# Block-causal attention and a SoLU layer on one core: transposed probabilities by way of DRAM, the first batch element in two parts, loads of two pairs at once

## The chip, the core and the metric

The kernel runs on one core of a Trainium2 chip: TensorE (PE), VectorE (DVE), ScalarE (ACT), GpSimd (POOL) and SyncE (SP), each with its own queue of instructions, and 16 DMA engines that carry the transfers. Nearly all transfers are issued on SP's queue. The metric is the device time of one execution in microseconds. Before: a median of 732.68 us over three runs (730.88 to 734.18).

## The reference

```python
# attention: 8 batch elements, 8 heads, 576 positions, head size 64; float32
scores = scale * np.matmul(q, k.transpose(0, 1, 3, 2))
mask = block_i >= block_j                  # blocks of 64 positions
scores = np.where(mask, scores, -1000000000.0)
attn = np.exp(scores - max); attn = attn / (sum + 1e-09)
attn_out = np.matmul(attn, v)
# then each of 4608 tokens, x = the 8 heads side by side (512)
h = x @ w_in                               # 512 -> 1024
solu = h * softmax(h)
ln = (solu - mean) / np.sqrt(var + 1e-06) * g_ln
out = ln @ w_out                           # 1024 -> 512
```

## The kernel before

Work comes in two kinds. **Attention** is done for a pair of heads at a time, 32 pairs, four to a batch element. **MoE tiles** (the SoLU layer) take 128 tokens each, 36 tiles, four and a half to a batch element; a tile can start when the attention output of its tokens stands in `xt`.

A product of float32 numbers is split into a high and a low part (`qh`, `ql`; `xh`, `xl`; `wih`, `wil` and so on) and made of three matmuls (L515, L673, L733). For a pair: q and k are loaded (L432, eight transfers of 32 partitions, each 18 runs of 32 numbers), transposed on DVE in 32x32 blocks (L474) and split; scores go to PSUM (L515, L509), DVE takes the row maximum (L540), ACT the exponential into `pb` (L552), and rows are scaled by the reciprocal of their sum (L570 to L572, on whichever of three engines is planned). The product with v needs the probabilities transposed, `pt`. DVE transposes `pb` within 32x32 blocks (L579); what is left is to move blocks between groups of 32 partitions, and that is `place` (L581 to L584): sixteen transfers of 32 partitions, 3,200 bytes per partition, from `pb` to `pt`, both in SBUF. The product with v (L596) then reads `pt`. The first four pairs (`PEP`, `PEQ`) are transposed on PE instead (L461, L496), while the weights are prepared from their 64-bit words (`prep`, L341).

For a MoE tile: h on PE (L673), maximum, exponential and product on DVE and ACT (L679 to L681), centring by POOL or DVE (L683), and again a transposition: DVE transposes u in 32x32 blocks into `zb` (L703, reading every fourth number), `zb` is written to the DRAM tile `zd` (L704) and read back rearranged into `ct` (L705), split into `ch` and `cl` (L711 to L715) and multiplied with w_out (L733). Tiles 0 to 3 and 35 use PE's transposition.

The order of the instructions on every engine is fixed when the program is built. A planner (`Schedule`, L59) plays the operations through with durations that are written beside them, and at each step gives an engine the ready operation with the lowest key; keys are the pair's or the tile's number plus an offset from `PARAMS`. `pb`, `pt` and `vr` have two buffers each. Transfers wait in SP's queue in its order: one that must wait holds those behind it.

Of the kernel before, what the change touches and what calls it, by code (L numbers as in the profile page):

```python
# [11 lines left out]
F32 = mybir.dt.float32  # L12
# [19 lines left out]
NPT = 2  # L32
PEP = (0, 1, 2, 3)
PET, PEL = 4, 35
NQK = 1
XB = 3
PEQ = 4
SWITCH = 70.0
SLACK = 120.0
START = {"PE": 0.0, "ACT": 2930.0, "DVE": 0.0, "POOL": 2500.0, "SP": 560.0}  # L40
PARAMS = {
# [6 lines left out]
    "a_w": 189.2, "a_xh": -137.2, "a_xl": -269.8, "a_c": -179.5, "a_o": 359.2, "np": 32, "l0": -21.1,  # L48
    "a_cl": -237.6, "a_ai": 1.9, "aff": 91.5, "a_t3": -207.8, "a_cm": -19.8, "a_cg": 177.6, "a_sa": -259.0,
    "a_sa32": -169.6, "a_qh": 4.5, "a_kl": -157.5, "a_ch": -224.1, "a_chd": 241.9, "a_clo": -32.4,  # L50
    "ct0": -156.5,
# [7 lines left out]
class Schedule:  # L59
# [49 lines left out]
    def run(self):  # L109
# [20 lines left out]
        while events:  # L130
# [18 lines left out]
            for e in engs:  # L149
# [46 lines left out]
                if best.dma > 0.0:  # L196
                    done = dmafree = max(done, dmafree) + best.dma
# [9 lines left out]
def kernel(  # L207
# [43 lines left out]
    qz, kz, qt, kt = (sb(x, [S]) for x in ("qz", "kz", "qt", "kt"))  # L251
    kq = sb("kq", [P])
# [20 lines left out]
    ub = [sb(f"ub{i}", [DFF]) for i in range(2)]  # L273
# [4 lines left out]
    zd = dp.tile([P, DFF], F32, name="zd")  # L278
    ct = sb("ct", [4, NKO, 32])
# [55 lines left out]
    w_in_w = w_in.bitcast(U32).rearrange("(c p) (n t) -> p c n t", p=P, t=2)  # L335
    w_out_w = w_out.bitcast(U32).rearrange("(c p) (n t) -> p c n t", p=P, t=2)
# [3 lines left out]

    def prep(i, src, hi, lo, gcol, name, key):  # L341
        raw = ub[i % 2].bitcast(U32).rearrange("p (n t) -> p n t", t=2)
        T1, T2, T3 = wtmp[i % 2]
        kr_, k1, k2, k3 = ("ub", i % 2), ("w1", i % 2), ("w2", i % 2), ("ob", i % 2)
        op("SP", 640, lambda: SP.dma_start(raw, src), w=[kr_], key=key, tail=2700, dma=1270)
# [22 lines left out]
    op("SP", 500, lambda: SP.dma_start(gt, g_ln.rearrange("(c p) -> p c", p=P)), w=["gt"], key=K["w0"] + K["w1"] * 6, tail=2100)  # L368
    n = 0
    for hf in range(2):  # L370
        for c in range(NKI):
            s_ = slice(hf * 512, hf * 512 + 512)
            prep(n, w_in_w[:, c, s_, :], wih[:, c, s_], wil[:, c, s_], None, f"wi{c}_{hf}", K["w0"] + K["w1"] * n)
            n += 1
    for c in range(NKO):
        prep(n, w_out_w[:, c, :, :], woh[:, c, :], wol[:, c, :], gt[:, c : c + 1], f"wo{c}", K["w0"] + K["w1"] * n)
        n += 1

    ptc = [(0, 4), (4, 8), (8, 12), (12, 16), (16, 19), (19, 22), (22, 25)]
# [3 lines left out]
    groups = [  # L383
        ("S", [(2, 0), (0, 384)], [320, 448]),
        ("S", [(1, 0)], [192]),
        ("S", [(3, 0)], [448]),
        ("D", [LAST], None),
    ]
    order_u = [(h, i) for is_ in ((2, 0), (1,)) for h in range(2) for i in is_] + [(0, 3), (1, 3), LAST]
# [16 lines left out]
    def attention(p):  # L406
        b0, hp = divmod(p, NP)
        i = p % 2
        sfx = "32" if p < NP else ""
# [3 lines left out]
        peq = p < PEQ  # L413
        pep = p in PEP
        for nm, src, dst in (("kz", k, kz), ("qz", q, qz)):

            def load(nm=nm, src=src, dst=dst):
                dma = ACT if p == 0 and nm == "kz" else SP
                if peq:
                    for h in range(2):  # L420
                        dma.dma_start(
                            dst[:, 0:512].rearrange("p (c d) -> p c d", c=4)[:, :, 64 * h : 64 * h + 64],
                            src[b0, 2 * hp + h, 0:512, :].rearrange("(c p) d -> p c d", p=P),
                        )
                    r0 = 0 if nm == "kz" else 64
                    SP.dma_start(
                        kq[r0 : r0 + 64, :].rearrange("p (h d) -> p h d", h=2),
                        src[b0, 2 * hp : 2 * hp + 2, 512:576, :].rearrange("h p d -> p h d"),
                    )
                    return  # L430
                for g in range(4):
                    dma.dma_start(  # L432
                        dst[32 * g : 32 * g + 32, :].rearrange("p (g d) -> p g d", d=32),
                        src[b0, 2 * hp + g // 2, :, 32 * (g % 2) : 32 * (g % 2) + 32].rearrange("(g p) d -> p g d", p=32),
                    )

            op("SP", 1790 if peq else 2040, load, w=[nm] + [nm + "q"] * peq, key=(K["l0"] if p == 0 else p) + K["ld" + sfx], tail=1700, dma=1870)
# [346 lines left out]
```

## Time and profile before

| | |
|---|---|
| median of three runs | 732.68 us |
| the profiled execution | 730.28 us, of which the span is 728.5 us |
| busy: PE, DVE, ACT, POOL | 92%, 83%, 68%, 44% of the span |
| DMA queue of SP (q1) | 230,416 packets, 124.32 MB, 70.1% of 16 engines |
| placing transfers `pt<-pb` | 448 (28 pairs x 16), from 88.4 to 639.5 us |
| weights and transposition on PE | until 88 us; MoE matmuls begin at 82.4 us |

In the rows that follow, a group's columns are its line, engine, operation, output and input tiles and count, then busy time and the mean of one in ns, then the engine's idle time before it and what ended it. In a row of windows the columns are the stretch in us, its length, the busy time of PE, PE's weight loads, DVE, ACT and POOL with their instructions, the granted clock of PE, the busy share of the 16 DMA engines and what they moved in GB/s. SPq is SP's queue, which issues transfers. The recorded ends of matmuls are modelled, so that PE's busy time is rather too high than too low.

### The profile page before, as it was taken

The numbers are of one execution on the slowest core, as the hardware profiler recorded it, in microseconds if no ns is written. First come the engines' busy times: TensorE is split into PE (matmuls) and PEld (weight loads), VectorE is DVE, ScalarE is ACT, GpSimd is POOL, SyncE is SP. The second block draws the span as 40 slices with busy tenths as digits, with TensorE's granted clock in tenths as the row PEclk, the third lists the DMA queues.
The fourth block names the chain that finished last, engine by engine and source line by source line (L and its number), as shares of the span: only waits on it lengthen the run. The fifth ranks groups of instructions, "written<-read, shape, count | busy, mean of one in ns | idle before, by whom it ended". The sixth has DMA issues, their size and how long they took to land.

```text
span 728.5 us, 14348 instructions
## 1 busy us (share of the span) xinstructions
PE 671.1 (92%) x4543; PEld 528.1 (72%) x4543; DVE 607.4 (83%) x1262; ACT 495.3 (68%) x1265; POOL 322.5 (44%) x491
## 2 busy tenths in 40 slices
PE   7786968999999998999999999899899988999997
PEld 6566757777677776778777777677677766878886
DVE  6999999988888999789799888899888789755672
ACT  5989958877777777665777686578585658434342
POOL 3755744454444655244353654245454434214310
PEclk7899989999999999999999999999999999999999
DMA  9584676676788888888778888888787874543431
GB/s 236 130 175 118 150 178 117 126 170 146 161 201 201 205 196 193 198 192 210 182 193 197 203 196 173 190 199 196 193 209 178 190 197 110 170 151 130 145 131 57
DMA packets 231547, 125.49 MB, mean 172 GB/s; under 512 B 190640, under 2 KB 206512, under 8 KB 231472
## 3 DMA queue, kind: packets, MB, share of 16 engines
q1 hardware_dynamic: 230416, 124.32, 70.1%
q8 instruction: 36, 0.59, 0.4%
q10 hardware_dynamic: 1056, 0.26, 0.2%
q14 instruction: 39, 0.32, 0.2%
HBM read 52.96 MB, written 25.69 MB: 108 GB/s over the span
## 4 chain that ended last, share of the span: by engine, by line
PE 32%; DVE 23%; SPq 14%; DMA 12%; ACT 12%; issue 5%; POOL 1%; DVEq 0%; ACTq 0%; POOLq 0%
PE ps L733 12%; SPq L584 11%; PE ps L673 9%; PE ps L596 5%; DVE pb L579 5%; DVE nm L540 5%; DMA pt<-pb 4%; ACT pb L552 4%; PE ps L515 4%; DMA ct<-zd 3%; ACT pb L572 3%; SPq L432 2%; DVE ub L681 2%; DVE zb L703 2%; PE ps L509 1%
## 5 line engine op out<-in xcount | busy, mean ns | idle before, releaser
L552 ACT ACTIVATE pb<-ps,nm 128x384 f32<-128x384 f32 (+4 forms) x288 | 157.3, 561 | 69.6 <-DVE nm L540 54.2
L540 DVE TENSOR_REDUCE nm<-ps 128x1 f32<-128x384 f32 (+4 forms) x288 | 131.8, 506 | 0.3
L596 PE MATMUL ps<-pt,vr 128*64 128x128 f32 (+2 forms) x1664 | 104.3, 286 | 25.4 <-DMA pt<-pb 13.7
L596 PEld LDWEIGHTS ps<-pt,vr 128*64 128x64 f32 x1664 | 90.2, 146 | 46.9 <-issue 16.4
L572 ACT ACTIVATE pb<-pb,rz 128x128 f32<-128x128 f32 (+4 forms) x191 | 101.2, 595 | 25.4 <-DVE rz L563 23.0
L579 DVE STREAM_TRANSPOSE pb<-pb 128x1536 f32<-128x1536 f32 (+1 forms) x56 | 102.1, 1829 | 9.5 <-POOL pb L570 5.8
L570 POOL TENSOR_SCALAR pb<-pb,rz 128x384 f32<-128x384 f32 (+4 forms) x97 | 62.3, 652 | 71.3 <-DVE rz L563 30.4
L733 PE MATMUL ps<-woh,ch 128*128 128x512 f32 x288 | 81.6, 405 | 4.0 <-ACT pb L552 3.4
L673 PE MATMUL ps<-wih,xh 128*128 128x512 f32 x288 | 83.8, 413 | 0.2 <-ACT xh L648 0.2
L673 PE MATMUL ps<-wil,xh 128*128 128x512 f32 x288 | 79.4, 398 | 0.0
L733 PE MATMUL ps<-woh,cl 128*128 128x512 f32 x288 | 78.7, 395 | 0.0
L673 PE MATMUL ps<-wih,xl 128*128 128x512 f32 x288 | 78.6, 395 | 0.0
L733 PE MATMUL ps<-wol,ch 128*128 128x512 f32 x288 | 78.6, 394 | 0.0
L733 PEld LDWEIGHTS ps<-woh,ch 128*128 128x128 f32 x288 | 51.8, 188 | 20.2 <-ACT pb L552 5.6
L703 DVE STREAM_TRANSPOSE zb<-ub 128x1024 f32<-128x1024 f32 x31 | 62.5, 2017 | 2.6 <-POOL ub L683 1.4
L673 PEld LDWEIGHTS ps<-wil,xh 128*128 128x128 f32 x288 | 54.8, 190 | 13.0
L673 PEld LDWEIGHTS ps<-wih,xh 128*128 128x128 f32 x288 | 51.1, 190 | 17.3 <-issue 4.8
L673 PEld LDWEIGHTS ps<-wih,xl 128*128 128x128 f32 x288 | 54.3, 188 | 12.8
L733 PEld LDWEIGHTS ps<-woh,cl 128*128 128x128 f32 x288 | 54.3, 188 | 12.8
L515 PE MATMUL ps<-kh,qh 64*128 64x384 f32 (+3 forms) x256 | 57.8, 390 | 6.2 <-ACT pb L552 1.8
L733 PEld LDWEIGHTS ps<-wol,ch 128*128 128x128 f32 x288 | 54.2, 188 | 12.7
L712 POOL TENSOR_SCALAR ch<-ct 128x512 fp32r<-128x512 f32 x36 | 22.0, 620 | 90.0 <-DMA ct<-zd 77.0
(116 smaller groups left out, 1262.3 us busy)
## 6 DMA issues: line engine op xcount, KB each, us to landing
pt<-pb SPq DMA_DIRECT2D x448, 100.0 KB, 2.2
zd<-zb SPq DMA_DIRECT2D x31, 512.0 KB, 3.0
ct<-zd SPq DMA_DIRECT2D x31, 512.0 KB, 4.3
out_dram<-ob SPq DMA_DIRECT2D x36, 256.0 KB, 3.1
vr<-in_v_dram SPq DMA_DIRECT2D x64, 128.0 KB, 3.3
kz<-in_k_dram SPq DMA_DIRECT2D x112, 72.0 KB, 2.7
qz<-in_q_dram SPq DMA_DIRECT2D x112, 72.0 KB, 3.0
ub<-in_moe_w_in_dram SPq DMA_DIRECT2D x8, 512.0 KB, 4.2
```

The lines of the kernel that those rows point to most:

```text
L515: PE.matmul(PS(sps[h])[:, off : off + 128 * (i_ + 1)], w_[half[h], 128 * i_ : 128 * i_ + 128], x_[half[h], 0 : 128 * (i_ + 1)], start=n_ = ...
L540: op("DVE", t_dve(wid[u]), lambda sp=sp, off=off, u=u: DVE.tensor_reduce(out=nm_[u], in_=PS(sp)[:, off : off + wid[u]], axis=AX.X, op=ALU. ...
L552: ACT.activation(dst, src, AF.Exp, bias=nm_[u], accum_out=z_[zg][:, zc : zc + 1])
L570: op("POOL", 0.836 * nn + 243, lambda b=b, zg=zg, zc=zc: POOL.tensor_scalar(out=puv(pb, b, pep), in0=puv(pb, b, pep), scalar1=rz_[zg][:, z ...
L572: ("ACT", t_act(nn, 93), lambda b=b, zg=zg, zc=zc: ACT.activation(puv(pb, b, pep), puv(pb, b, pep), AF.Copy, scale=rz_[zg][:, zc : zc + 1] ...
L579: op("DVE", 1.058 * 128 * (s1 - s0) + 86, lambda s0=s0, s1=s1: DVE.transpose(pb[:, :, s0:s1, :], pb[:, :, s0:s1, :]), r=[("P", i, b) for b ...
L584: SP.dma_start(pt_[32 * r_ : 32 * r_ + 32, a_, :, :], pb[32 * a_ : 32 * a_ + 32, r_, :, :])
L596: PE.matmul(dst(PS(av)[half[h]]), vt[:, j, 64 * h : 64 * h + 64], pt_[:, a0:a1, sl, :], start=start, stop=stop)
L673: PE.matmul(o_, a_[:, c, :], w_[:, c, s_], start=(si == 0 and c == 0), stop=(si == 2 and c == NKI - 1))
L703: op("DVE", t_dve(DFF), lambda: DVE.transpose(zb.rearrange("p (r c i) -> p r c i", r=4, i=32), u.rearrange("p (c i r) -> p r c i", r=4, i= ...
L712: alts=[("POOL", 671, lambda c_=c_, h_=h_: POOL.tensor_scalar(out=h_, in0=c_, scalar1=1.0, scalar2=1.0, op0=ALU.mult, op1=ALU.mult), K["a_ ...
L733: PE.matmul(o_, a_[:, c, :], w_[:, c, :], start=(hf == 0 and si == 0 and c == 0), stop=(hf == 1 and si == 2 and c == 7))
```

## The change

1. *Transposed probabilities by DRAM.* `place` goes. In its stead four writes (`spill`) bring `pb`, 128 partitions wide each, to a DRAM tile `pd` (two buffers), in the order that `pt` needs, and one read brings the whole of it to `pt`, 12,800 bytes per partition. The read waits until the four writes have landed.
2. *Two-pair loads.* q and k of two pairs are loaded by four transfers of 36 runs instead of eight of 18; to make these regular, a pair is now made of heads `ha` and `ha + 2`, and rows of w_in are loaded in the order that fits. DVE transposes them in place.
3. *First batch element in two parts.* For its four pairs, positions 0 to 255 are done first (`part` 0) and the other 320 after (`part` 1), with transposition on PE in both; MoE tiles 0 and 1 can start after the first part.
4. *W_out rows permuted.* With the rows of w_out and g_ln in another order, DVE's transposition of u into `zb` reads runs of 32 neighbouring numbers instead of every fourth. Tiles 0 to 3 and 35, transposed on PE, have their centred u written to `zb` in that order. w_in and w_out are fetched two blocks at a time.
5. *New priorities.* All of `PARAMS` is new, and the planner counts the time of the DMA queue otherwise (`DEPTH`).

The diff, cut to its core:

```diff
+DEPTH = 2500.0
-                    done = dmafree = max(done, dmafree) + best.dma
+                    dmafree = max(t + min(best.dur, 600.0), dmafree) + best.dma
+                    engfree[e] = max(done, dmafree - DEPTH)
+                    done = max(engfree[e], dmafree)
...
+    pd = [dp.tile([P, 4 * NSL * 32], F32, name=f"pd{i}") for i in range(2)]
...
+    def load2(nm=nm, src=src, dst=dst):
+        for g in range(4):
+            SP.dma_start(
+                dst[32 * g : 32 * g + 32].rearrange("p m (g d) -> p (m g) d", d=32),
+                src[b0, ha + g - g % 2 : ha + g - g % 2 + 2, :, 32 * (g % 2) : 32 * (g % 2) + 32].rearrange("m (g p) d -> p (m g) d", p=32),
+            )
+    if part is None and zs == 0:
+        op("SP", 3000, load2, w=[(nm, 0), (nm, 1)], key=lk, tail=1700, dma=4000)
...
+    groups_of = {
+        None: [("S", [(2, 0), (0, 384)], [320, 448]), ("S", [(1, 0)], [192]), G3, GL],
+        0: [("S", [(1, 0), (0, 256)], [192, 320])],
+        1: [G2, G3, GL],
+    }
...
-        def place():
-            for r_ in range(4):
-                for a_ in range(4):
-                    SP.dma_start(pt_[32 * r_ : 32 * r_ + 32, a_, :, :], pb[32 * a_ : 32 * a_ + 32, r_, :, :])
...
-            op("SP", 16 * 633, place, r=[("T", i, 0), ("T", i, 1)] + [("P", i, u) for u in units], w=ptk, key=p + K["pe" + sfx], tail=1500, dma=250)
+            pd_ = pd[p % 2]
+
+            def spill():
+                for r_ in range(4):
+                    SP.dma_start(pd_[32 * r_ : 32 * r_ + 32].rearrange("j (a n) -> a j n", a=4), pb[:, r_].rearrange("p s i -> p (s i)"))
+
+            op("SP", 4 * 590, spill, r=tk, w=[("pd", p % 2)], key=p + K["pe" + sfx], tail=1800, dma=4000)
+            op("SP", 590, lambda: SP.dma_start(pt_.rearrange("p a s i -> p (a s i)"), pd_), r=[("pd", p % 2)], w=ptk, key=p + K["pe" + sfx], tail=1800, dma=4000)
...
-        if PET <= t < PEL:
-            op("DVE", t_dve(DFF), lambda: DVE.transpose(zb.rearrange("p (r c i) -> p r c i", r=4, i=32), u.rearrange("p (c i r) -> p r c i", r=4, i=32)), r=[uk] + (wkeys if t == PET else []), w=["zb"], key=key + K["ct"])
+        if t in BT:
+            op("DVE", t_dve(DFF), lambda: DVE.transpose(zb.rearrange("p (r c i) -> p r c i", r=4, i=32), u.rearrange("p (c r i) -> p r c i", r=4, i=32)), r=[uk] + (wkeys if t == BT[0] else []), w=["zb"], key=key + K["ct"])
...
+    for part in range(2):
+        for p in range(NP):
+            attention(NP * part + p, p, part)
+        tiles((256, S)[part])
+    for p in range(NP, K["np"]):
+        attention(NP + p, p)
```

Where the instructions stand now, in two places. The first is **SP's queue in the middle of the program**, over one pair before and over two pairs after. A row is the line, the operation, its tiles, the size of the output (outermost dimension first) and a count of equal rows. Before:

```order
L432 DMA kz<-in_k_dram 32x18x32 x4
L432 DMA qz<-in_q_dram 32x18x32 x4
L705 DMA ct<-zd 128x4x256
L584 DMA pt_93<-pb_91 32x800 x16
L704 DMA zd<-zb 128x1024
L441 DMA vr_84<-in_v_dram 128x4x64 x2
L445 DMA vr_84<-in_v_dram 64x2x64
L739 DMA out_dram<-ob_138 128x512
```

After, in lines of the changed kernel (652 the writes, 655 the read, 464 the loads of q and k, 788 and 789 `zd` and `ct`, 823 the store):

```order
L652 DMA pd_130<-pb_88 4x32x800 x4
L475 DMA vr_81<-in_v_dram 128x4x64 x2
L479 DMA vr_81<-in_v_dram 64x2x64
L464 DMA qz<-in_q_dram 32x36x32 x4
L655 DMA pt_90<-pd_130 128x3200
L823 DMA out_dram<-ob_136 128x512
L652 DMA pd_131<-pb_89 4x32x800 x4
L788 DMA zd<-zb 128x1024
L823 DMA out_dram<-ob_135 128x512
L655 DMA pt_91<-pd_131 128x3200
L789 DMA ct<-zd 128x4x256
```

Between a pair's writes and its read stand at most the loads of v and q or a store and a `zd`; behind the read stand the store, the next pair's writes and `zd`. The destination of a write has 4 as its outermost dimension, its source 128 partitions; all other transfers have 32, 64 or 128 on both sides.

The second is **PE's queue at the end of the program**, from the last pair's product with v on. Before, 54 groups of four matmuls for the output (L733) and 30 for h (L673) stand behind it; it begins so:

```order
L596 MATMUL ps_66<-pt_94,vr_84 64x2x2x32 x8
L596 MATMUL ps_66<-pt_94,vr_84 64x64 x10
L733 MATMUL ps_64<-woh,ch 128x512 x4
L733 MATMUL ps_64<-wol,ch 128x512 x4
L733 MATMUL ps_64<-woh,cl 128x512 x4
```

After, 66 for the output (L817) and 45 for h (L751):

```order
L665 MATMUL ps_65<-pt_91,vr_81 64x2x2x32 x8
L665 MATMUL ps_65<-pt_91,vr_81 64x64 x10
L817 MATMUL ps_64<-woh,ch 128x512 x4
L817 MATMUL ps_64<-wol,ch 128x512 x4
L817 MATMUL ps_64<-woh,cl 128x512 x4
```

The h of two and a half tiles more, and the output of two, now stand behind the last product.

More of the change, by code (lines that the diff above doesn't have):

```diff
@@ L32 @@
 NPT = 2
[L33 to L34 removed]
+PEP = tuple(range(8))
+BT = tuple(range(4, 35))
 NQK = 1
 XB = 3
[L37 removed]
 SWITCH = 70.0
+DEPTH = 2500.0
 SLACK = 120.0
@@ L272 @@
     xl = [sb(f"xl{i}", [NKI, P], F32R) for i in range(2)]
-    ub = [sb(f"ub{i}", [DFF]) for i in range(2)]
+    ub2 = sb("ub", [2, DFF])
+    ub = [ub2[:, i] for i in range(2)]
     zb = sb("zb", [DFF])
@@ L404, in puv, with fetch0, attention @@
         return pb[:, :, soff[u] : soff[u] + u[1] + 1, :]
-    def attention(p):
-        b0, hp = divmod(p, NP)
+    raw0 = [xt[1 + x].rearrange("p a n -> p (a n)") for x in range(2)]
+    chv = qz.rearrange("p z n -> p (z n)")
+    tail0 = kz[:, 0]
+    def fetch0():
+        for c in range(5):
+            for x, src in enumerate((k, q)):
+                if c < 4:
+                    dst, src = raw0[x][:, 512 * c : 512 * c + 512], src[0, :, P * c : P * c + P, :]
+                else:
+                    dst, src = tail0[64 * x : 64 * x + 64, 0:512], src[0, :, 512:S, :]
+                eng = ACT if c == 0 and x == 0 else SP
+                op("SP", 600, lambda eng=eng, dst=dst, src=src: eng.dma_start(dst.rearrange("p (h d) -> p h d", d=64), src.rearrange("h p d -> p h d")),
+                   w=[("raw", x, c)], key=2 * c - 2000 if c < 2 else K["l0"] + K["ld32"] + 4 * c, tail=1700, dma=1150)
+            if c < 2:
+                op("SP", 600, lambda c=c: SP.dma_start(chv[:, 512 * c : 512 * c + 512].rearrange("p (h d) -> p h d", d=64), v[0, :, P * c : P * c + P, :].rearrange("h p d -> p h d")),
+                   w=[("v0", c)], key=c - 1990, tail=1700, dma=1150)
+    fetch0()
+    def attention(p, pair, part=None):
+        b0, hp = divmod(pair, NP)
         i = p % 2
-        sfx = "32" if p < NP else ""
+        sfx = "A" if part == 0 else "32" if p < 2 * NP else ""
+        groups, zlast = groups_of[part], zlast_of[part]
+        mine = [u for u in units if part is None or (u[1] < 2) == (part == 0)]
+        slots = [s_ for u in mine for s_ in range(soff[u], soff[u] + u[1] + 1)]
         pb, vt, pt_ = pbs[i], vr[i], ptb[p % NPT]
@@ new lines, in attention @@
+        for x, z, hi, lo, scale in () if peq or part == 0 else (("k", kz[:, zs], kh_, kl_, 1.0), ("q", qz[:, zs], qh_, ql_, 0.125)):
+            zk = (x + "z", zs)
+            op("DVE", t_dve(S) + 30, lambda z=z: DVE.transpose(z, z), r=[zk], w=[zk], key=kk)
+            op("ACT", t_act(S), lambda z=z, hi=hi, scale=scale: ACT.activation(hi, z, AF.Copy, scale=scale), r=[zk], w=[(x + "h", iq)], key=ke,
+               alts=[("POOL", 0.836 * S + 243, lambda z=z, hi=hi, scale=scale: POOL.tensor_scalar(out=hi, in0=z, scalar1=scale, scalar2=1.0, op0=ALU.mult, op1=ALU.mult), K["a_qh"])])
@@ L741, with tiles @@
     done = 0
-    for p in range(K["np"]):
-        attention(p)
+    def tiles(tokens):
+        nonlocal done
+        while (done + 1) * P <= tokens:
+            moe(done, (NP + K["h0"] if done > 3 else K["hA"]) + done * K["hs"])
+            done += 1
+    for part in range(2):
[4 more added lines that the diff above has]
+        attention(NP + p, p)
         if p % NP == NP - 1:
-            tokens = (p // NP + 1) * S
-            while (done + 1) * P <= tokens:
-                moe(done, NP + K["h0"] + done * K["hs"])
-                done += 1
+            tiles((p // NP + 1) * S)
     with tc.manual_schedule():
```

222 lines of the change are left out of this document (127 added, 95 removed), and 12 rows, old and new, of the table PARAMS.

## The prediction

> **What bounds the kernel now.** I began with the page's busy shares and the chain of work that ended last.
>
> ```profile
> span 728.5 us, 14348 instructions
> PE 671.1 (92%) x4543; PEld 528.1 (72%) x4543; DVE 607.4 (83%) x1262; ACT 495.3 (68%) x1265; POOL 322.5 (44%) x491
> PE 32%; DVE 23%; SPq 14%; DMA 12%; ACT 12%; issue 5%; POOL 1%; DVEq 0%; ACTq 0%; POOLq 0%
> ```
>
> No engine stands alone: PE is the busiest, but two thirds of the chain lie elsewhere, 14% of it on SP's queue. That mean hides three stages, so the windows come next: the head (to the first placing of probabilities at 88 us), the middle (all 28 placed pairs), the tail, and three short stretches used below.
>
> ```profile
> core 0: us, PE busy (x) PEld busy (x) DVE busy (x) ACT busy (x) POOL busy (x), PEclk, DMA share, GB/s
> ...
> 88.00:640.00 552.00, 516.98 (x3586) 405.66 (x3585) 481.50 (x991) 385.28 (x1001) 251.52 (x376) 0.98 0.77 182
> 640.00:728.50 88.50, 83.97 (x404) 67.75 (x402) 48.39 (x80) 33.91 (x60) 20.23 (x30) 1.00 0.35 122
> 660.00:680.00 20.00, 20.00 (x88) 16.22 (x87) 13.06 (x21) 9.04 (x16) 7.63 (x8) 1.00 0.37 132
> 664.00:668.00 4.00, 4.00 (x19) 3.25 (x18) 1.53 (x6) 3.51 (x6) 3.81 (x4) 1.00 0.34 137
> 318.00:325.00 7.00, 6.74 (x43) 5.44 (x42) 6.78 (x16) 3.80 (x15) 1.96 (x3) 1.00 0.74 162
> ```
>
> The middle takes 552 us for 28 pairs, 19.7 us each. There PE is busy for 517 us (94%), DVE for 87%, and all 16 DMA engines for 77% of the time. PE has at most 35 us of visible idleness to give back; DMA has the next thinnest margin, and this change leans on DMA. The tail is matrix work alone: 88 matmuls in 20 us, 227 ns each.
>
> Last, SP's instructions in order of time over one pair (start, us, line, transfer, count).
>
> ```profile
> 308.25 2.64 SPq L432 DMA_DIRECT2D qz<-in_q_dram  x4
> 310.93 2.13 SPq L432 DMA_DIRECT2D kz<-in_k_dram  x4
> 313.16 0.45 SPq L705 DMA_DIRECT2D ct<-zd  x1
> 313.70 1.01 SPq L441 DMA_DIRECT2D vr<-in_v_dram  x2
> 314.76 0.66 SPq L445 DMA_DIRECT2D vr<-in_v_dram  x1
> 315.52 10.69 SPq L584 DMA_DIRECT2D pt<-pb  x16
> 326.31 0.53 SPq L704 DMA_DIRECT2D zd<-zb  x1
> ```
>
> And from the view of line 584, what one placing costs in issue (least, median, most, in ns) and how long it takes to land (us):
>
> ```profile
> L584 SPq DMA_DIRECT2D pt<-pb x448: 507/591/2012, 88.4 to 639.5; - x150
> ...
> DMA to landing us min/median/max: 2.1/2.2/6.5
> ```
>
> SP issues without a gap: one pair's sixteen placings alone hold it for 10.69 us of every 19.7. That is the cost which the change attacks.
>
> **The change part by part: the round trip through DRAM.** Gone are 16 issues per pair at a median of 591 ns; in come five, so SP gets back about 11 x 0.6 = 6.6 us per pair. What it pays is DMA time. First the present bill, per engine and pair: 0.77 x 552 / 28 = 15.2 us. Of this the placings: 1.64 MB (16 x 102.4 KB) at the rate of the stretch 318 to 325 us, in which almost only they ran (162 GB/s at a share of 0.74, so 219 GB/s for all 16 engines), are 7.5 us. The other 7.7 us (q, k, v, the MoE tiles' transfers) stay, since the same bytes move.
>
> ```profile
> pt<-pb SPq DMA_DIRECT2D x448, 100.0 KB, 2.2
> zd<-zb SPq DMA_DIRECT2D x31, 512.0 KB, 3.0
> ct<-zd SPq DMA_DIRECT2D x31, 512.0 KB, 4.3
> ```
>
> The read back, 128 rows of 12.8 KB, has as its nearest row the write of zd, which had the stretch 664 to 668 us to itself: 137 GB/s at a share of 0.34, so 403 GB/s for 16 engines, 25.2 for one. 1.64 MB are then 4.1 us per engine.
>
> The four writes are the unknown. By the orders shown above, every transfer of the kernel before begins, on both sides, with a dimension of 32, 64 or 128; each write begins with 128 on the source and with 4 on the destination (4 x 32 x 800). If a transfer is dealt out to the engines along its outermost dimension, in shares that both sides have in common, a write has four shares and runs on four engines of the sixteen. No view of the trace shows the dealing, so both ends stand: on 16 engines the four writes cost each engine 4.1 us per pair at zd's rate (7.5 at the placings'); on four they cost those four 1.64 MB / 4 / 25.2 GB/s = 16.3 us (29.9 at the placings' 13.7 GB/s an engine) and the other twelve nothing. I take four engines, because 4 is the only count that the outermost dimensions 4 and 128 share with sixteen, and zd's rate, because zd's is the write into DRAM. I take further that all four writes meet the same four engines, because their access patterns differ only in offset.
>
> [...]
>
> So for the four loaded engines a pair is 7.7 + 4.1 + 16.3 = 28.1 us, above the 19.7 that a pair takes now, and 28 pairs are 787 us. DMA becomes the bound of the middle.
>
> **The added wait.** The read stands in SP's queue behind a wait for the four writes to land; queued behind it are the out stores, the next pair's writes, zd and ct. The smallest landing, 2.1 us for a transfer whose moving takes some 0.5, says a landing costs about 1.6 us after the last byte. Loads of v and q issued ahead of the read keep the engines busy for part of it; I add 1 us per pair: 28. Bounds: nothing, and 2 x 28 = 56.
>
> **Tail.** The matmuls standing after the last attention product are 45 groups of four for h and 66 for the output, against 30 and 54: 444 x 227 ns = 101 us instead of 336 x 227 = 76. The tail grows by these 25 us, from 88 to 113: PE, which waits for DMA in the middle, could have done them there, but the order of its instructions is fixed.
>
> **Edits costed at nothing.** The transpose into zb now reads runs instead of every fourth element.
>
> ```profile
> L703 DVE STREAM_TRANSPOSE zb<-ub 128x1024 f32<-128x1024 f32 x31 | 62.5, 2017 | 2.6 <-POOL ub L683 1.4 <-DMA zd<-zb 0.8
> L579 DVE STREAM_TRANSPOSE pb<-pb 128x1536 f32<-128x1536 f32 x28 | 49.3, 1761 | 6.3 <-POOL pb L570 5.8 <-ACT pb L572 0.2 <-DMA pt<-pb 0.2
> ```
>
> At the 1.15 ns an element of the pb transpose it would take 1.17 us: up to 31 x 0.84 = 26 us of DVE saved, at worst none. In the forecast DVE idles behind DMA and nothing comes of it. Two-pair loads spare SP four issues a pair (about 2 us), hidden for the same reason. Splitting the first batch element brings the first MoE matmuls forward on PE and adds transposes; the head ends when the first pair is written out, and I leave it at 88 us (bounds 70 to 95). The permuted weights change only loads in the head. Five tiles write their centred u into zb in permuted order, on POOL or DVE: 0 to 5 us, taken as 0 beside the head's slack. The new priorities carry no price of their own; they are what put the tail's matmuls there.
>
> **Sum:** 88 + 787 + 28 + 113 = 1016 us of span. The profiled execution before had 730.28 us for its span of 728.5 and the runs a median of 732.68; with these 4 us: **1020 us**. Its own range: from 940 (head 70, no waits, tail 88) to 1120 (write rows a quarter slower, which is 4 us a pair).
>
> **Rivals.** *A: the writes spread over all 16 engines (faster).* A pair is 7.7 + 4.1 + 4.1 = 15.9 us of DMA, under 19.7, SP is half free, and the middle falls back on PE, of whose 35 idle us I give it 30: 698 of span, 702 us, 670 to 718 as DVE's relief comes through or not. For it: SP's gapless stretch and 14% of the chain. Against: the shape of the destination. It decides from eight engines on: there the writes are 8.1 us and a pair 19.9, which is today's. *B: 16 engines, but both halves of the round trip move as slowly as the placings.* 7.7 + 7.5 + 7.5 = 22.7 us a pair, 28 x 3.0 = 84 us longer: 817 us. For it: two transfers each moving what one did. Against: zd's 403 GB/s into the same DRAM. *C: the change doesn't do what it says*: SP's relief is real, but a wait on two landings in series replaces it in front of the attention products, and the time stays: 733 us. Against: the order puts two pairs' products behind the scores of the next two, which leaves some 40 us for the trip.
>
> **How the numbers follow.** Forecast 0.66, A 0.25, B 0.04, C 0.05: two in three because the destination's 4 is the one thing in which these transfers differ in kind from all that the trace holds, and no more than that because no row shows the dealing itself. What a measurement can tell from no change here is about 0.5%. The forecast and B are slower: 0.70; C splits into 0.03 same and 0.01 to each side; A is faster but for 0.01: faster 0.25, same 0.04, slower 0.71. Range: the forecast's 940 to 1120 holds about 0.61; down to 695 it takes in B, C and half of A: 695 to 1120.
>
> **What would show it.** Right: the DMA share of the middle falls, though its time grows (busy engine time per pair 15.9 x 16 over 28 us: about 0.56); pd<-pb lands over 15 us after its issue, the read in 5 to 8; PE below 75% busy there, waiting for pt<-pd, the chain mostly DMA. Wrong: pd<-pb landing in 4 to 6 us, and a DMA share of 0.75 or more. The zb transpose shows by its mean, 1.2 or 2.0 us. The forecast fails if the dealing isn't by the outermost dimension, or if each write takes other engines.

## The result and the profile after

The changed kernel takes a median of **1089.53 us** (four runs, 1086.23 to 1094.13) against 733.43 us before (four runs): a ratio of **1.485**, 95% interval 1.475 to 1.495. The forecast was 1020 us, with 940 to 1120 as its own range: the side and the mechanism hold, and 70 us are missing in the sizes.

First the head of the profiled execution's page: span, instructions, the busy share of each engine and its number of instructions; then SP's DMA queue (packets, MB, share of 16 engines) and the chain of work that ended last, by engine and by line.

```profile
span 1090.6 us, 14173 instructions
PE 743.1 (68%) x4747; PEld 585.2 (54%) x4747; DVE 581.7 (53%) x1291; ACT 486.2 (45%) x1257; POOL 337.5 (31%) x502
q1 hardware_dynamic: 227984, 170.69, 54.3%
DMA 29%; PE 23%; SPq 16%; ACT 4%; DVE 2%; issue 2%; POOL 0%; ACTq 0%; DVEq 0%; POOLq 0%
DMA zd<-zb 13%; PE ps L817 9%; SPq L464 8%; PE ps L751 6%; DMA pd<-pb 5%; PE ps L665 5%; DMA out_dram<-ob 5%; DMA ct<-zd 4%; SPq L479 3%; SPq L652 3%; SPq L475 2%; PE ps L576 2%; DVE zb L787 1%; ACT pb L617 1%; ACT pb L637 1%
```

The queue moves 170.69 MB instead of 124.32, yet its share falls from 70.1% to 54.3%. PE, the busiest before, has fallen to 68% of the span. The row accounts for 76% of the span; DMA and SP's queue have 45 of these 76, and the largest piece is not the new transfer: it is the unchanged write of zd.

The windows of the three stages, the head in two rows (stretch, length, busy time of PE, weight loads, DVE, ACT, POOL, granted clock, DMA share, GB/s):

```profile
0.00:30.00 30.00, 16.27 (x133) 13.00 (x133) 11.42 (x37) 14.33 (x41) 6.62 (x18) 0.73 0.92 186
30.00:127.00 97.00, 84.04 (x698) 66.13 (x699) 86.47 (x209) 87.43 (x232) 58.57 (x78) 0.89 0.49 103
127.00:970.00 843.00, 533.63 (x3413) 417.83 (x3411) 428.42 (x939) 343.79 (x916) 236.54 (x363) 0.79 0.57 168
970.00:1090.60 120.60, 109.14 (x504) 88.20 (x504) 55.36 (x108) 40.68 (x71) 35.76 (x45) 0.95 0.33 121
```

The middle runs from the first write of probabilities to the last read back: 843 us for 28 pairs, 30.1 us each, with PE busy 63% of the time and DMA at 0.57. Most of the time is lost there: 552 us became 843.

The chain of waits in order of time (start, us, what), in a stretch of the middle:

```profile
516.97 7.85 DMA out_dram<-ob
526.04 15.98 DMA zd<-zb
...
542.47 1.25 DVE zb L787
...
565.71 3.45 SPq L475
569.21 3.74 SPq L479
...
579.21 7.21 DMA out_dram<-ob
587.35 16.51 DMA zd<-zb
```

And SP's queue over the same stretch (start, us of issue, line, transfer, count):

```profile
517.45 8.49 SPq L652 DMA_DIRECT2D pd<-pb  x4
526.04 3.59 SPq L788 DMA_DIRECT2D zd<-zb  x1
529.73 1.79 SPq L823 DMA_DIRECT2D out_dram<-ob  x1
540.92 0.32 SPq L655 DMA_DIRECT2D pt<-pd  x1
...
549.24 0.34 SPq L788 DMA_DIRECT2D zd<-zb  x1
...
553.65 0.56 SPq L789 DMA_DIRECT2D ct<-zd  x1
555.19 6.26 SPq L652 DMA_DIRECT2D pd<-pb  x4
561.56 7.60 SPq L475 DMA_DIRECT2D vr<-in_v_dram  x2
569.21 3.74 SPq L479 DMA_DIRECT2D vr<-in_v_dram  x1
573.00 5.13 SPq L464 DMA_DIRECT2D qz<-in_q_dram  x4
578.18 0.93 SPq L655 DMA_DIRECT2D pt<-pd  x1
579.21 0.38 SPq L823 DMA_DIRECT2D out_dram<-ob  x1
579.69 7.55 SPq L652 DMA_DIRECT2D pd<-pb  x4
```

Two pairs pass in 62 us (517.45 to 579.69). The write of zd, 3.0 us before, takes 16 us when it is issued behind four writes of probabilities (526.04). The next zd (549.24) has no such writes ahead of it, and its reading back (ct) is issued 4.4 us later, so it had landed by then. The last stretch before the slow one lands shows what it waits for:

```profile
535.00:541.00 6.00, 1.16 (x6) 0.59 (x4) 0.00 (x0) 0.00 (x0) 0.00 (x0) 0.87 0.26 103
```

The writes, zd and a store have been issued by then and haven't landed, and the share is 0.26, as much as four of the 16 engines (0.26 x 16 = 4.2); the read of probabilities can be issued only at 540.92. No view shows single engines. I read the share as about four that still hold a long queue and twelve that have nothing left, while the mean of the middle says that DMA is little more than half busy. A low mean share beside unchanged transfers that land five times later is how an uneven load looks in these views. SP suffers from it too: two loads of v, which issued in 1.01 us before, hold it for 7.60.

### The profile page after: what moved, and what is told of

Read it like the earlier page. It is cut to its first block, busy times and chain, and to the rows that moved or that the text cites. A ratio compares the mean times of both kernels' runs of the same rounds, so it can differ in the third digit from the quotient of the medians.

```text
span 1090.6 us, 14173 instructions
## 1 busy us (share of the span) xinstructions
PE 743.1 (68%) x4747; PEld 585.2 (54%) x4747; DVE 581.7 (53%) x1291; ACT 486.2 (45%) x1257; POOL 337.5 (31%) x502
## 3 DMA queue, kind: packets, MB, share of 16 engines
q1 hardware_dynamic: 227984, 170.69, 54.3%
## 4 chain that ended last, share of the span: by engine, by line
DMA 29%; PE 23%; SPq 16%; ACT 4%; DVE 2%; issue 2%; POOL 0%; ACTq 0%; DVEq 0%; POOLq 0%
DMA zd<-zb 13%; PE ps L817 9%; SPq L464 8%; PE ps L751 6%; DMA pd<-pb 5%; PE ps L665 5%; DMA out_dram<-ob 5%; DMA ct<-zd 4%; SPq L479 3%; SPq L652 3%; SPq L475 2%; PE ps L576 2%; DVE zb L787 1%; ACT pb L617 1%; ACT pb L637 1%
## 5 line engine op out<-in xcount | busy, mean ns | idle before, releaser
L665 PE MATMUL ps<-pt,vr 128*64 128x128 f32 (+1 forms) x1648 | 122.3, 318 | 155.4 <-ACT pb L617 67.5
L617 ACT ACTIVATE pb<-ps,nm 128x256 f32<-128x256 f32 (+4 forms) x288 | 157.1, 561 | 116.3 <-DMA pd<-pb 67.1
L576 PE MATMUL ps<-kh,qh 64*128 64x128 f32 (+3 forms) x256 | 67.5, 439 | 136.7 <-ACT qh L536 74.8
L637 ACT ACTIVATE pb<-pb,rz 128x384 f32<-128x384 f32 (+4 forms) x179 | 95.1, 592 | 118.0 <-DVE rz L628 117.3
L605 DVE TENSOR_REDUCE nm<-ps 128x1 f32<-128x256 f32 (+4 forms) x288 | 131.1, 505 | 0.3
L576 PEld LDWEIGHTS ps<-kh,qh 64*128 64x128 f32 x256 | 34.6, 223 | 164.2 <-ACT qh L536 78.3
L635 POOL TENSOR_SCALAR pb<-pb,rz 128x128 f32<-128x128 f32 (+4 forms) x79 | 46.6, 602 | 210.6 <-DVE rz L628 167.7
L787 DVE STREAM_TRANSPOSE zb<-ub 128x1024 f32<-128x1024 f32 x31 | 38.1, 1229 | 121.2 <-DMA zd<-zb 114.1
L817 PE MATMUL ps<-woh,ch 128*128 128x512 f32 x288 | 83.3, 412 | 25.4 <-ACT pb L617 25.4
L751 PE MATMUL ps<-wih,xh 128*128 128x512 f32 x288 | 90.7, 440 | 0.0
L751 PE MATMUL ps<-wil,xh 128*128 128x512 f32 x288 | 82.8, 411 | 0.0
L817 PE MATMUL ps<-wol,ch 128*128 128x512 f32 x288 | 80.6, 402 | 0.0
L817 PE MATMUL ps<-woh,cl 128*128 128x512 f32 x288 | 79.1, 397 | 0.0
L751 PE MATMUL ps<-wih,xl 128*128 128x512 f32 x288 | 78.7, 395 | 0.0
L817 PEld LDWEIGHTS ps<-woh,ch 128*128 128x128 f32 x288 | 54.1, 194 | 41.7 <-ACT pb L617 25.8
L769 ACT ACTIVATE ob<-ub 128x1024 bf16<-128x1024 f32 x31 | 32.8, 1057 | 95.4 <-DMA out_dram<-ob 74.8
L535 DVE STREAM_TRANSPOSE qz<-qz 128x576 f32<-128x576 f32 x28 | 20.1, 756 | 97.6 <-DMA qz<-in_q_dram 97.6
L751 PEld LDWEIGHTS ps<-wil,xh 128*128 128x128 f32 x288 | 58.5, 203 | 14.4
L751 PEld LDWEIGHTS ps<-wih,xh 128*128 128x128 f32 x288 | 56.0, 208 | 15.5 <-issue 3.0
L817 PEld LDWEIGHTS ps<-wol,ch 128*128 128x128 f32 x288 | 55.8, 194 | 13.4
```

The costliest lines, as they stand in the source:

```text
L576: PE.matmul(PS(sps[h])[:, off : off + 128 * (i_ + 1)], w_[half[h], 128 * i_ : 128 * i_ + 128], x_[half[h], 0 : 128 * (i_ + 1)], start=n_ = ...
L605: op("DVE", t_dve(wid[u]), lambda sp=sp, off=off, u=u: DVE.tensor_reduce(out=nm_[u], in_=PS(sp)[:, off : off + wid[u]], axis=AX.X, op=ALU. ...
L617: ACT.activation(dst, src, AF.Exp, bias=nm_[u], accum_out=z_[zg][:, zc : zc + 1])
L635: op("POOL", 0.836 * nn + 243, lambda b=b, zg=zg, zc=zc: POOL.tensor_scalar(out=puv(pb, b, pep), in0=puv(pb, b, pep), scalar1=rz_[zg][:, z ...
L637: ("ACT", t_act(nn, 133), lambda b=b, zg=zg, zc=zc: ACT.activation(puv(pb, b, pep), puv(pb, b, pep), AF.Copy, scale=rz_[zg][:, zc : zc + 1 ...
L665: PE.matmul(dst(PS(av)[half[h]]), w_, pt_[:, a0:a1, sl, :], start=start, stop=stop)
```

## Experiments

### Is it the number of engines that a write is dealt to?

Two kernels share the changed kernel's order on every engine. One turns the trip round: `pb` is written as it lies, 128 rows outermost, and the rearrangement is done by four reads.

```diff
             def spill():
+                SP.dma_start(pd_, pb.rearrange("p r s i -> p (r s i)"))
+
+            def fetch(pd_=pd_):
                 for r_ in range(4):
-                    SP.dma_start(pd_[32 * r_ : 32 * r_ + 32].rearrange("j (a n) -> a j n", a=4), pb[:, r_].rearrange("p s i -> p (s i)"))
+                    SP.dma_start(pt_[32 * r_ : 32 * r_ + 32].rearrange("p a s i -> p a (s i)"), pd_[:, 800 * r_ : 800 * r_ + 800].rearrange("(a j) n -> j a n", a=4))
...
```

> The changed kernel with the same bytes by the same DRAM tile, the same five issues per pair and the same order on every engine; only the shapes differ: one write of 128 rows as pb lies, then four reads whose outermost dimension is 32 on both sides. Theory (a transfer is dealt out along its outermost dimension; the four writes run on four engines): every transfer now has all 16, a pair needs about 16 us of each engine, and the middle falls back to PE: 670 to 740 us, a pair in about 19 to 20 us. Rival 1 (the loss is the wait for two landings in series in SP's queue): the read still waits for the write, so still 1000 us or more. Rival 2 (the DRAM round trip's bytes are too many for 16 engines at the old placings' rate): about 820 us.

The other halves the outermost dimension: each write is cut into two whose destination begins with 2 instead of 4.

```diff
                 for r_ in range(4):
-                    SP.dma_start(pd_[32 * r_ : 32 * r_ + 32].rearrange("j (a n) -> a j n", a=4), pb[:, r_].rearrange("p s i -> p (s i)"))
+                    for z_ in range(2):
+                        SP.dma_start(pd_[32 * r_ : 32 * r_ + 32, 1600 * z_ : 1600 * z_ + 1600].rearrange("j (a n) -> a j n", a=2), pb[64 * z_ : 64 * z_ + 64, r_].rearrange("p s i -> p (s i)"))
```

> The changed kernel with each of the four writes cut into two of 64 partitions, so that the destination's outermost dimension is 2 instead of 4; the bytes, the DRAM tile, the read and the order stay. Theory: two engines carry all writes, 1.64 MB / 2 / 25.2 GB/s = 32.5 us per pair instead of 16.3, so a pair takes about 16 us more than in the changed kernel: 1089 + 28 x 16 = about 1540 us. Rivals 1 and 2 (landings in series, or bytes): about 1090 us, up to 1160 if the four more issues per pair (0.6 us each) are exposed.

Measured: **818.4 us** with 128 outermost (1.118 times before, 1.114 to 1.121), and **1506 us** with 2 (one execution). Windows of the middle: of the one write; then of the eight, with four microseconds in which little but their writes is under way:

```profile
120.00:670.00 550.00, 479.33 (x3290) 373.71 (x3290) 417.92 (x928) 339.03 (x903) 234.03 (x358) 0.93 0.99 247
```

```profile
300.00:1200.00 900.00, 392.73 (x2458) 307.21 (x2458) 313.87 (x681) 247.70 (x661) 177.71 (x269) 0.70 0.38 115
630.00:634.00 4.00, 4.00 (x48) 3.40 (x42) 1.24 (x2) 0.00 (x0) 0.00 (x0) 1.00 0.13 52
```

The same bytes give a DMA share of 0.38 with 2 outermost, 0.57 with 4 and 0.99 with 128. Where the writes are alone, the share is 0.13 with 2, as much as an eighth of the engines, at 52 GB/s; with 4 it was 0.26 at 103 GB/s in the changed kernel. By these shares they are two and four engines, at some 26 GB/s each. Several writes of a pair are under way at once, so by the share they meet the same engines; other ones for each write would have made it larger. Which engines they are, no view shows. The step from four to two costs (1506 - 1090) / 28 = 14.9 us a pair. If the writes cost each of four engines W/4, they cost each of two W/2, so that the difference is W/4 itself: 14.9 us against the 16.3 of the forecast.

The 818 us miss the 670 to 740 of my theory, though: a second limit, with the DMA share at 0.99, stands behind the first. It comes after the next experiment.

### The trip in the order of before

To see the trip without the rest of the change: the kernel before, its own order, `place` alone replaced by four writes and a read as in the changed kernel.

```diff
         def place():
+            pd_ = pd[p % 2]
             for r_ in range(4):
-                for a_ in range(4):
-                    SP.dma_start(pt_[32 * r_ : 32 * r_ + 32, a_, :, :], pb[32 * a_ : 32 * a_ + 32, r_, :, :])
+                SP.dma_start(pd_[32 * r_ : 32 * r_ + 32].rearrange("j (a n) -> a j n", a=4), pb[:, r_].rearrange("p s i -> p (s i)"))
+            SP.dma_start(pt_.rearrange("p a s i -> p (a s i)"), pd_)
```

> The kernel before, in its own order, with only the sixteen placings replaced by the change's four writes and one read. Theory (this one part carries the whole loss): the middle goes from 19.7 us a pair to between 28 and 31: 728 + 28 x 8.4 to 28 x 11.3, 963 to 1045 us. Rival 3 (the new order and the other parts cost the time): within 20 us of 733.

Measured: **1173 us** (one execution), more than expected. SP's queue over one pair and the beginning of the next, and a window in which little but the second pair's writes is under way, tell why:

```profile
502.65 4.65 SPq L585 DMA_DIRECT2D pd<-pb  x4
523.63 0.35 SPq L586 DMA_DIRECT2D pt<-pd  x1
...
542.73 4.67 SPq L585 DMA_DIRECT2D pd<-pb  x4
564.87 0.35 SPq L586 DMA_DIRECT2D pt<-pd  x1
```

```profile
549.00:561.00 12.00, 5.31 (x27) 3.32 (x25) 8.77 (x19) 6.65 (x20) 2.79 (x4) 0.93 0.26 102
```

Nothing is issued between writes and read here, so the writes are seen alone: a share of 0.26, as much as a quarter of the engines, at 102 GB/s. 1.64 MB at that rate are 16.1 us. The read comes 21.0 us after the first write's issue begins and 16.3 after the last one's ends (523.63 - 507.30); 22.1 and 17.5 in the next pair. This pair takes 40.1 us and the average one about 36 (the first write is issued at 89.0 us, the last at 1058.1), because the other transfers come after the landing instead of beside it. The trip alone therefore makes this kernel 440 us slower; the rest of the change isn't needed for the loss. In the changed kernel, where loads stand between writes and read, a pair takes 30.1.

### The second limit: where a read lands

In the kernel of 818 us a read lands on 32 neighbouring partitions. Next, the exponential writes the blocks of `pb` in the other order, and a read lands on every fourth partition; bytes, counts and order stay.

```diff
-                            src, dst = src.rearrange("p (c r i) -> p c r i", r=4, i=32), dst.rearrange("p r c i -> p c r i")
+                            src, dst = src.rearrange("p (c i r) -> p c r i", r=4, i=32), dst.rearrange("p r c i -> p c r i")
...
-                    SP.dma_start(pt_[32 * r_ : 32 * r_ + 32].rearrange("p a s i -> p a (s i)"), pd_[:, 800 * r_ : 800 * r_ + 800].rearrange("(a j) n -> j a n", a=4))
+                    SP.dma_start(pt_[r_::4].rearrange("p a s i -> p a (s i)"), pd_[:, 800 * r_ : 800 * r_ + 800].rearrange("(a j) n -> j a n", a=4))
```

> The changed kernel with one write of 128 rows and four reads, as in one_write_four_reads (818 us, DMA share 0.99 in its middle, its 3.2 KB read rows slow), but the exponential writes its blocks in another order (every fourth column of scores to one r), so that each read lands on every fourth partition instead of 32 neighbouring ones. [...] Rival (reading rows of 3.2 KB from DRAM is slow of itself): 810 to 825 us.

Measured: **764.8 us** (1.045 times before, 1.040 to 1.050), 54 us less, and below the rival's 810 to 825; with the reads at the write's rate, 15.9 us of each engine a pair, my estimate was 740 to 785. The DMA issues (transfer, count, KB each, us from issue to landing) of the kernel with neighbouring partitions:

```profile
pd<-pb SPq DMA_DIRECT2D x28, 1600.0 KB, 8.0
pt<-pd SPq DMA_DIRECT2D x112, 400.0 KB, 7.3
```

and of that with every fourth, with windows of its middle and tail:

```profile
pd<-pb SPq DMA_DIRECT2D x28, 1600.0 KB, 8.3
pt<-pd SPq DMA_DIRECT2D x112, 400.0 KB, 5.2
```

```profile
125.00:640.00 515.00, 476.32 (x3382) 373.80 (x3384) 422.20 (x941) 344.91 (x915) 239.13 (x365) 0.96 0.93 273
640.00:762.00 122.00, 116.30 (x550) 93.79 (x546) 56.13 (x108) 41.49 (x74) 35.79 (x45) 1.00 0.37 129
```

The read's landing falls from 7.3 to 5.2 us, and DMA moves 273 GB/s at a share of 0.93 instead of 247 at 0.99: 18% more per busy engine. By these windows the 32 us that are still lost against before stand in the head (125 us against 88) and the tail (122 against 88.5). The middle takes 515 us against 552, with fewer matmuls in it (3382 against 3586), since the new order puts more of them into the head and the tail. Why a read onto neighbouring partitions lands later was not shown, and the rate of one read alone, no view gives.

The same two trips in the order of before, where the write and the reads stand next to each other on SP, are the control. Of `place`, one line:

```diff
+            SP.dma_start(pd_, pb.rearrange("p r s i -> p (r s i)"))
```

and the four reads onto neighbouring partitions, or onto every fourth as above.

> The kernel before, in its own order, with the sixteen placings replaced by one write of 128 rows and four reads of 32 partitions, all dealt to 16 engines by the theory. Theory: SP is held for about 0.6 + 5.7 (write and landing) + 4 x 0.6 = 8.7 us per pair instead of 10.7, in the same order: 715 to 735 us. Rivals 1 and 2: 28 times a wait of 6 us or more on the path, 800 us or more.

> The kernel before in its own order, with one write of 128 rows and four reads onto every fourth partition (the exponential's blocks ordered for it). Theory: the rest of the 99 us by which before_with_one_write was over the kernel before was the slow reads and the wait for them: 725 to 760 us. Rival (the two landings in series on SP's queue, which this order doesn't cover): 800 us or more.

Measured: **831.9 us** (1.137, 1.132 to 1.142) and **795.9 us** (1.087, 1.080 to 1.093; four executions, 791.8 to 804.6). Spreading is worth some 36 us here too; both totals miss my theory, which forgot that in this order SP stands through the landing of every write (174 us in all in the first kernel, 172 in the second) and PE waits for the reads (99 and 50 us). The chain of the first by line, and most of its middle:

```profile
DMA pt<-pd 16%; DMA pd<-pb 16%; PE ps L598 8%; PE ps L735 7%; DMA out_dram<-ob 5%; SPq L433 4%; PE ps L675 4%; DMA zd<-zb 4%; ACT pb L553 3%; DVE nm L541 3%; DVE zb L705 3%; SPq L586 2%; DVE pb L580 2%; PE ps L516 2%; ACT pb L573 1%
88.00:640.00 552.00, 453.42 (x3046) 357.42 (x3044) 417.58 (x858) 338.29 (x877) 222.50 (x332) 0.93 0.89 227
```

A third of the chain is the two landings, while DMA is at 0.89: bandwidth is not all that binds here.

The kernel before, replanned with write and reads as two operations, so that other transfers stand between them, with spread reads, other priorities, and the DMA queue's time counted as in the changed kernel:

```diff
+            op("SP", 400, spill, r=[("T", i, 0), ("T", i, 1)] + [("P", i, u) for u in units], w=[("pd", p % 2)], key=p + K["pe" + sfx], tail=1900, dma=4000)
+            op("SP", 4 * 560, fetch, r=[("pd", p % 2)], w=ptk, key=p + K["pf"], tail=1800, dma=4300)
```

> The kernel before with the trip through DRAM on sixteen engines, one write and four reads onto every fourth partition, the two planned as separate operations and the order of all engines planned anew with other priorities, so that other transfers stand between the write and the reads on SP. If what the trip costs in the order of before (796 us) was SP standing still between the two, this recovers it: 725 to 760. If DMA, at nearly full load, is what binds it: 760 to 790.

Measured: **742.0 us** (1.014, 1.011 to 1.017): SP's wait for the writes falls from 172 us to 38, and most of the standing still is recovered; which of the things replanned did it was not taken apart. Its middle:

```profile
100.00:640.00 540.00, 503.55 (x3560) 396.01 (x3559) 455.30 (x945) 381.30 (x981) 248.17 (x376) 0.98 0.88 266
```

Even so the trip doesn't beat sixteen placings: SP is relieved, but DMA goes from 0.77 to 0.88 and PE gains nothing.

### What the other parts of the change are worth

*The transposition into zb.* From the kernel of 764.8 us, with the old access pattern again (the rows of w_out stay permuted, so that tiles 4 to 34 multiply rows that don't belong to them; of the line, the part that differs):

```diff
-u.rearrange("p (c r i) -> p r c i", r=4, i=32)
+u.rearrange("p (c i r) -> p r c i", r=4, i=32)
```

> The kernel four_spread_reads with the transposition into zb reading every fourth number again (2.02 us instead of 1.23 us each), all else alike, so that its tiles 4 to 34 multiply w_out's rows in an order that doesn't fit and those rows of the output differ from the reference. Theory (DVE is not the bound): 31 x 0.79 = 24 us more DVE, at most 10 us more time. Rival (the transposition is on the path of each tile): 15 to 25 us more.

And the reverse in the kernel before: the new pattern alone, with the rows of w_out in their old order.

> The kernel before with one access pattern changed: DVE's transposition into zb reads runs of 32 neighbouring numbers, with no rows of w_out permuted, so that the output of tiles 4 to 34 differs from the reference and only the time counts. In this kernel DVE is busy for 87% of the middle and stands in 23% of the chain. If the 0.79 us by which one transposition is cheaper reach the end where DVE is near the limit, up to 24 us go: 708 to 725. If, as in the kernels with a trip through DRAM, it is worth nothing: 730 to 735.

Measured: **764.2 us** against 764.8, nothing; and **727.5 us** against 732.8 in the kernel before (0.994, 0.992 to 0.997), 5 us less. The transposition's row with the new pattern in the kernel before:

```profile
L703 DVE STREAM_TRANSPOSE zb<-ub 128x1024 f32<-128x1024 f32 x31 | 38.1, 1230 | 2.4 <-POOL ub L683 1.4 <-DMA zd<-zb 0.7
```

Of 31 x 0.79 = 24 us, where DVE is busy for 87% of the middle, a fifth reaches the end; in the kernel of 764.8 us, with DMA at 0.93 in the middle, none does.

*The rest, without the trip.* The changed kernel with the sixteen placings put back and the planner run on it:

```diff
+                    for a_ in range(4):
+                        SP.dma_start(pt_[32 * r_ : 32 * r_ + 32, a_, :, :], pb[32 * a_ : 32 * a_ + 32, r_, :, :])
...
+            op("SP", 16 * 633, place, r=tk, w=ptk, key=p + K["pe" + sfx], tail=1500, dma=250)
```

> The changed kernel with the sixteen placings of the kernel before in the stead of the DRAM round trip; two-pair loads, the first element in two parts, permuted w_out and the new priorities stay, and the planner orders anew. Theory (the round trip is the loss, the other parts are near zero together): 715 to 760 us. Rival 3 (the new order or the head in two parts costs 30 us or more of itself): 760 to 800 us.

Measured: **833 us** (1.139, 1.133 to 1.145; two executions), above all that I expected. Since the planner orders everything anew for other durations with priorities that were not made for them, this is no clean price of the other parts; I take from it only that priorities and operations belong together. Its placings run from 127.5 to 734.1 us, so the late start, at least, is not in the trip but in the rest of the change (the first write of the kernels with the changed order comes at 126.8 to 127.6 us, whatever its shape):

```profile
L651 SPq DMA_DIRECT2D pt<-pb x448: 507/592/1668, 127.5 to 734.1; - x150
```

### A version that beats both

A read landed in 7.3 us on neighbouring partitions and in 5.2 on spread ones; a placing, which lands on 32 neighbouring ones, might gain too. In the kernel before, its order untouched, the exponential's blocks are turned as above, and a placing lands on every fourth partition:

```diff
-                    SP.dma_start(pt_[32 * r_ : 32 * r_ + 32, a_, :, :], pb[32 * a_ : 32 * a_ + 32, r_, :, :])
+                    SP.dma_start(pt_[r_::4, a_, :, :], pb[32 * a_ : 32 * a_ + 32, r_, :, :])
```

> The kernel before, its order of instructions unchanged, its sixteen placings kept (no trip through DRAM); only what they touch is turned: the exponential writes the blocks of pb in the other order, and a placing lands on every fourth partition of pt instead of 32 neighbouring ones. If a transfer runs at half rate because of the neighbouring partitions at one end, and the other ends of transfers in flight do not matter much, a pair's placings take 4.1 to 6 us of an engine's time instead of 7.5, the DMA share of the middle falls from 0.77 to between 0.60 and 0.70, and the time falls by 0 to 12 us (SP's issue, unchanged, is then what is left): 718 to 733. If the source, still 32 neighbouring partitions, sets the rate, the share stays at 0.75 or above and the time within 3 us of before.

Measured: **728.6 us** against 732.8 (0.994, 0.992 to 0.997): 0.6% faster than before, with two lines. The interval leaves out 1, but 4 us is small: the medians of the kernel before in the several sets of runs lie between 730.8 and 733.4. Its middle, and the stretch in which almost only placings ran:

```profile
88.00:640.00 552.00, 519.80 (x3611) 408.05 (x3612) 486.21 (x993) 385.75 (x1002) 251.85 (x378) 0.98 0.73 184
318.00:325.00 7.00, 7.00 (x36) 5.21 (x34) 6.90 (x19) 5.03 (x18) 1.46 (x3) 1.00 0.54 139
```

The DMA share falls from 0.77 to 0.73, between the two theories' numbers: 0.04 x 552 / 28 = 0.8 us a pair of the 7.5 that the placings cost. In the short stretch 16 engines would move 139 / 0.54 = 257 GB/s, against 219 before. The source is still 32 neighbouring partitions; whether this end now sets the rate was not shown, since a placing with both ends spread was not tried.

Last, both gains in one whole kernel, with w_out permuted and the order planned anew.

> The kernel before with the two edits that helped it kept together, whole again: placings onto every fourth partition, and the zb transposition that reads runs, with the rows of w_out and g_ln permuted as in the changed kernel and the centred u of tiles 0 to 3 and 35 written in that order to one buffer of its own, which orders these tiles; the order of all engines is planned anew with other priorities for it. If the two gains (4 us each in before's own order) add and the new order costs nothing: 722 to 728. If a new order costs what the replanned orders so far have cost (9 us and more): 733 to 745.

Measured: **731.7 us** against 730.8 (1.002, 0.999 to 1.004): no difference, between the two expectations. The transposition is at its 1228 ns and the DMA share at 0.74, so what made both gains is there. What takes them back was not taken apart: the order, the buffer added for tiles 0 to 3 and 35, or that the two don't add.

## Why the prediction was right, and where its sizes were off

**The dealing of the writes: right.** It was the one step on which the forecast stood against rival A, an assumption of mine from a dimension of 4, which no row of before showed. The shares of the writes alone, 0.26 with 4 outermost and 0.13 with 2, agree with it, and the eight writes and the one write show its price from both sides. That the DMA share of the middle, forecast at 0.56, is 0.57 is in part luck: the forecast's engine time over the 30.1 us that a pair took would be 15.9 / 30.1 = 0.53, and both the engine time and the pair came out longer.

**The writes' price: right.** Forecast 16.3 us a pair on each of four engines; 16.1 by the rate of the writes alone, 14.9 by the slope. In the changed kernel the read is issued 15.0 us after the last write (525.94 to 540.92), at the mark of the forecast, a landing over 15 us after the issue. The choice of zd's rate, and not of the placings', was the right one.

**The rest of a pair: too small.** 30.1 - 16.1 = 14.0 us (15.2 by the slope), where the sum had 7.7 + 4.1 + 1 = 12.8. The chain shows what the added wait left out: not only the read waits; every transfer issued behind the writes (zd, the store, loads of v and q) lands late or cannot be issued. PE, which I had expected to wait for pt<-pd, seldom does: of 309 us of idle PE in the middle, 38 ended with pt<-pd and most of the rest with ACT, while ACT, DVE and SP waited for late transfers (DVE 99 us for zd, 98 for q). How the 1.2 to 2.4 us divide between such waits and dearer transfers was not measured apart. An estimate from the mean share: of 0.57 x 16 x 30.1 = 274.5 us of engine time a pair the writes take 4 x 16.1; the rest is 13.1 us on each of 16 engines, where the sum had 7.7 + 4.1, and the four loaded ones would then idle for 0.9 us, close to the 1 us of wait. That 1 us leaned on an estimate, 2.1 - 0.5 = 1.6 us of a landing; where in a landing these lie, no view shows. Over 28 pairs the middle is 843 us against 815.

**The head: mis-sized, the largest error.** I left it at 88 us, with bounds of 70 to 95, and argued that the split brings MoE matmuls forward. They begin at 83.3 us (82.4 before), and the first write at 127.6. Before's head from 30 us on, to set beside the row of 30 to 127 us above; then groups of PE's instructions up to the first placing of before, and up to the first write of after:

```profile
30.00:88.00 58.00, 46.62 (x429) 37.05 (x429) 54.79 (x133) 54.56 (x149) 35.95 (x51) 0.91 0.58 131
```

```profile
L461 PE MATMUL ps<-ident,kz 128*128 128x128 f32 x16 | 3.1, 328 | 0.4 <-DMA kz<-in_k_dram 0.4
L461 PE MATMUL ps<-ident,qz 128*128 128x128 f32 x16 | 3.0, 318 | 1.2 <-ACT pb L552 1.1
L673 PE MATMUL ps<-wih,xh 128*128 128x512 f32 x8 | 2.4, 420 | 0.2 <-ACT xh L648 0.2
```

```profile
L490 PE MATMUL ps<-ident,xt 128*64 128x128 f32 x192 | 16.1, 328 | 0.1
...
L751 PE MATMUL ps<-wih,xh 128*128 128x512 f32 x20 | 6.8, 470 | 0.0
...
L817 PE MATMUL ps<-woh,ch 128*128 128x512 f32 x8 | 2.4, 416 | 0.0
```

Before, 8 matmuls of the first kind for h precede the first placing; after, 20 precede the first write, with output products beside them, so that the order, which I had read at two places only, puts the h of one and a half MoE tiles more, and the output of one, ahead of the first pair. The split of the first element costs too: 192 matmuls that transpose q and k take 16.1 us where before 32 took 6.1. How the 39 us divide stays open, and PE alone doesn't set the head: from 30 us on ACT is busy for 90% of the head, DVE for 89% and PE for 87%, and the first 30 us hold less work than before (DVE 11.4 us against 22.7).

**The tail: nearly right.** 120.6 us against 113: the matmuls that I counted are there (504 in this window against 404 in before's), with 11.5 us of PE idle in place of 4.5 and a granted clock of 0.95 instead of 1.00.

**Sum.** 39 + 28 + 8 = 75 us: 1016 of span forecast, 1090.6 measured. All three errors go the same way. The ends of the range are not quite the sums behind them: head 70, no waits and tail 88 give 949 instead of 940, and writes a quarter slower 1020 + 28 x 4 = 1132 instead of 1120; the result lies within either.

**Edits costed at nothing: the transposition, nearly so; the split and the order, not.** The last two stand in the head. The group of the zb transposition in the changed kernel:

```profile
L787 DVE STREAM_TRANSPOSE zb<-ub 128x1024 f32<-128x1024 f32 x31 | 38.1, 1229 | 121.2 <-DMA zd<-zb 114.1
```

Its mean is 1.23 us (1.17 forecast), and before it DVE idles 114.1 us for zd. What the saving is worth in this kernel was not tried; in the kernel of 764.8 us it was nothing. In the kernel before it is worth 5 us, less than the "up to 26 us saved" that I named as its cover's worth.

**The rivals.** *A*, 16 engines at zd's rate, gave 702; with 16 engines on the write the kernel took 818, and with reads spread too 765. It needed two things that it took for one: engines for the write, and spread partitions for the read. Then the middle takes 515 us, near the 552 - 30 = 522 that A gave it, and the rest of the 765 is the longer head and tail. *B* forecast 817 by both halves moving like placings. That 818 came from the kernel with one write is luck: B had 22.7 us a pair and the head and tail of before; that kernel takes about 20 us a pair and has the longer head and tail. What slowed it in B's sense was one half alone, the reads onto neighbouring partitions: 54 us of the whole. I had given B 0.04 because of zd's rate, and had not asked in what the placings differ from zd; the 219 against 403 GB/s in before's trace were the sign of it. *C*, a wait in the place of SP's time, is nearest to what the trip does when DMA is not starved: 742 us in the replanned order, 796 where nothing stands between write and reads.

## What to carry to other kernels

Before a rearrangement is moved into a DMA, write down the outermost dimension of both its sides and the partitions that it touches: here writes with 4 outermost had a DMA share of 0.26 where they were alone and those with 2 had 0.13, as much as four and two of 16 engines, and reads onto 32 neighbouring partitions landed later than onto 32 that are spread (7.3 against 5.2 us). In a profile, a low mean DMA share (0.57 here) with unchanged transfers landing several times later than before (zd 16 us against 3.0) may mean a few overloaded engines and not spare bandwidth; look at a short window in which only the suspect transfer is under way, as the one with 0.26 here. And when a program's order is planned, count what stands ahead of the first transfer of the changed stage, not only what stands behind the last.

## What the runs showed of the hardware that was not expected

- Halving the outermost dimension of a write (4 to 2) halved its rate, 102 to 52 GB/s at shares of 0.26 and 0.13 where the writes are alone: 14.9 us a pair more, at a mean DMA share of 0.38.
- Beside the writes with 4 outermost, unchanged transfers land late: zd 3.0 us to landing before, 16 to 16.5 in the chain of the changed kernel, and issues of SP stretched with it (two loads of v from 1.01 to 7.60 us).
- A read of 400 KB landed in 7.3 us on 32 neighbouring partitions and in 5.2 on every fourth: 54 us of the whole.
- The granted clock of PE was lower in the middles in which PE waits more: 0.98 in before's (PE busy 94%), 0.79 in the changed kernel's (63%), 0.70 with eight writes (44%). Whether it cost time there was not tried; of the matmuls for h, those of `wil` by `xh` took 414 ns on average in the changed kernel's middle and 398 in before's, those of `wih` by `xl` 395 in both.
